# V in SBUF at 136 instead of 130 bf16 per key chunk, in an attention and MLP kernel on one core

## The chip, the cores and the metric

The kernel runs on one core of a Trainium2 chip. The metric is the time of one execution on the device, in microseconds (us); the median of three runs is given with its lowest and highest. A core has engines that run side by side: PE (matrix products; it loads one operand, the weights, into its array, which the profile lists as PEld, and streams the other one through), DVE (vector work), ACT (activation functions), POOL and SP (here mostly issuers of DMAs). Data lie in SBUF, which has 128 partitions, and PE writes its results to PSUM.

## What is computed

```python
# x (1, 2048, 576), k_cache and v_cache (1, 16, 2048, 128), all bf16
xn = layernorm(x)
# A: 32 query heads on 16 key heads, of the last W = 512 keys
q = (xn @ wq) as 32 heads of 128
scores = q @ k.T * 128 ** -0.5
p = softmax(scores)
o = p @ v
s = o as (2048, 4096) @ wo
# B: an MLP block with a token shift
h = gelu(layernorm(xn) @ w1); hs = shifted(h) @ w2; x1 = xn + hs
b = x1 + gelu(layernorm(x1) @ w3) @ w4
out = x + s * silu(b)
```

## The kernel before

The 2048 tokens are cut into 4 query blocks of 512 (QB, NB). A unit u is one query block and one of the 32 query heads, so there are 128 units; two query heads share a key head g = (u % 32) // 2. The 512 keys of a key head are 4 chunks kc of 128 (KCH).

Attention is a loop over the units. In it `stage_q` makes the queries of the next unit (line 439, with a remainder at 425 from the second block on), `stage_s` the scores of this unit, chunk by chunk (line 459), from which ACT makes the exponentials pT in bf16 (line 461; a pool of 10 tiles), and `stage_v` weighs V for the unit before (line 476). For every token tile of 128, `stage_v` adds four matmuls, kc 0 to 3, into one place of `po`: the weights are a 128x128 piece of pT, and the streamed operand is 129 columns of V, of which the last is ones, so that column 128 of the result is the sum of the exponentials. The first of the four overwrites, the others add. Two token tiles share one `po` tile (2 of them, PSUM), so a call is eight matmuls, and there are 2 calls a unit, 256 in all, 2048 matmuls. DVE then takes the reciprocal of the sums and multiplies (lines 480, 481), and a DMA transposes the outcome (line 489).

Between these, PE is given pieces of other work by unit: transposes of K (line 297), the output projection of the block before (line 500, into `pswo` 512 columns wide and `pswr` 64 wide), and the first half of the MLP (lines 552 and 603). After the loop come the output projection of the last block, and the second half of the MLP (lines 849, 886 and, at the end, 1049 and 1069). The order on PE, POOL and SP in the attention part is the order of the program; the order on ACT and DVE is made by the framework's planner, which is told of some priorities.

V is kept in `v_sb`, one tile for all 16 key heads (line 215): on each partition 16 x 4 chunks of VW values, VW = Dh + 2 = 130 (line 77). A chunk's first 128 values are filled by DMA, 256 bytes a row (`load_v`, line 287): the first two calls on SP's queue at the start, the other six on POOL's, each eight units ahead of its first use. The remaining VW - 128 values of every chunk are set to 1.0 once, on POOL, at the start (line 330). `stage_v` reads values 0 to 128 of a chunk (line 477). On POOL the fills of line 331 to 333 (w1r_sb, w1_sb and w2_sb) and the V loads stand behind line 330.

```python
v_sb = res.tile([P, Hkv, KCH, VW], BF16, name="v_sb")                       # 215
nc.gpsimd.memset(v_sb[:, :, :, Dh:VW], 1.0)                                  # 330
nc.tensor.matmul(po[:, j, :], lhsT=pTs[kc][:, tt * P:(tt + 1) * P],          # 476
                 rhs=v_sb[:, g, kc, 0:Dh + 1], start=(kc == 0), stop=(kc == KCH - 1))
```

Of the kernel before, what the change touches and what calls it, by code (L numbers as in the profile page):

```python
# [31 lines left out]
def kernel(  # L32
# [19 lines left out]
    _, Hkv, Sk, Dh = A_k_cache.shape  # L52
# [21 lines left out]
    rsz = c4 - P  # L74
    SHIFT = [1, -1, 2, -2]
    PAD = 2
    VW = Dh + 2
    HP = 1500

    x2 = A_x.rearrange("b s d -> (b s) d")  # L80
# [127 lines left out]
    with ExitStack() as actx:  # L208
# [5 lines left out]
        kT = res.tile([P, Hkv, W], BF16, name="kT")  # L214
        v_sb = res.tile([P, Hkv, KCH, VW], BF16, name="v_sb")
        NWQ = 2
# [60 lines left out]
        def load_k(i, eng=None, step=4):  # L277
            kst_t[i] = x1_pool.tile([P, TB, D], BF16, name="x1")
            dst = kst_t[i][:].rearrange("p a b -> p (a b)")[:, 0:4 * W].rearrange("p (g a) -> p g a", g=4)
            for g in range(0, 4, step):  # L280
                (eng or nc.gpsimd).dma_start(
                    out=dst[:, g:g + step, :],
                    in_=A_k_cache[0, 4 * i + g:4 * i + g + step, K0:, :].rearrange("g (p kc) d -> p g (kc d)", p=P))
# [39 lines left out]
        with tc.manual_schedule(engines={SP}):  # L323
# [5 lines left out]
            load_k(1, nc.sync)  # L329
        nc.gpsimd.memset(v_sb[:, :, :, Dh:VW], 1.0)  # L330
        nc.gpsimd.memset(w1r_sb[:], 0.0)
# [866 lines left out]
```

## Time and profile before

| | us |
|---|---|
| median of three runs (lowest, highest) | 837.76 (837.19, 838.02) |
| profiled execution, its time | 837.62 |
| its span, first to last instruction | 835.8 |
| attention loop, first to last V matmul start | 15.4 to 514.0 |
| second half of the MLP on PE, from | 545.8 |

The granted clock of PE was 0.998 over the span. The profile is of one execution. Its page gives busy time by engine, the span in 40 slices with busy tenths, the costliest groups (line, engine, operation, result<-operands, shape, count, then busy us and the mean ns of one, then the engine's idle time ahead of them and what ended most of it), and the DMA queues. The trace also answers with a list of waits (engine, line and the event waited for: us in total, times, longest), with a timeline, where neighbouring instructions of one line are put together (start us, length us, count), and with windows (for a stretch: busy us of each engine, PE's clock, DMA share, GB/s). A matmul's length there is its passage through the array's pipeline, in which the next one already runs; how fast matmuls follow each other is read from their starts. A few records of matmuls are missing, none of line 476's.

### The profile page before, as it was taken

How to read it: one execution, taken by the hardware profiler on the slowest of the kernel's cores; microseconds unless marked ns; L12 is line 12 of the kernel's file. 1: busy time of each engine (PE TensorE's matmuls, PEld its weight loads, DVE VectorE, ACT ScalarE, POOL GpSimd, SP SyncE). 2: the span in 40 equal slices, each digit the busy share in tenths (PEclk: the TensorE clock that was granted, in tenths of full speed). 3: DMA queues.
4: the chain of work that ended last, by engine and by line, in shares of the span. 5: the costliest groups of instructions: out<-in, count | busy, mean ns of one | idle time of the engine just before them, and what ended most of it. 6: DMA issues, size and time to landing. Idle time of an engine off the chain costs nothing.

```text
span 835.8 us, 19469 instructions
## 1 busy us (share of the span) xinstructions
PE 820.3 (98%) x7885; PEld 475.9 (57%) x7971; DVE 473.8 (57%) x1430; ACT 452.9 (54%) x806; POOL 91.8 (11%) x157
## 2 busy tenths in 40 slices
PE   8999999999999999999999999999999999999997
PEld 5666654665554466655465655455555555555555
DVE  5778655568794366965346774044245636645333
ACT  6777763488783368984357983033332433334610
POOL 3242323011110101110000100000000000000000
PEclk9999999999999999999999999999999999999999
DMA  7988992263473135762035464992001411230101
GB/s 186 198 160 196 189 181 74 62 116 92 90 150 62 42 88 125 132 130 60 13 80 120 103 107 73 305 346 53 2 3 43 81 52 44 47 87 16 44 15 46
DMA packets 140752, 83.95 MB, mean 100 GB/s; under 512 B 107328, under 2 KB 133632, under 8 KB 140656
## 3 DMA queue, kind: packets, MB, share of 16 engines
q1 hardware_dynamic: 130048, 53.01, 31.3%
q0 software_dynamic: 9216, 28.15, 12.7%
q8 instruction: 64, 1.05, 0.6%
q10 hardware_dynamic: 1392, 1.48, 0.5%
q14 instruction: 32, 0.26, 0.1%
HBM read 49.17 MB, written 9.44 MB: 70 GB/s over the span
## 4 chain that ended last, share of the span: by engine, by line


## 5 line engine op out<-in xcount | busy, mean ns | idle before, releaser
L461 ACT ACTIVATE pT<-sc 128x512 bf16<-128x512 f32 x512 | 288.9, 596 | 116.1 <-PE sc L459 105.5
L459 PE MATMUL sc<-qT,kT 128*128 128x512 bf16 x493 | 169.0, 378 | 0.9 <-DVE qT L449 0.6
L476 PEld LDWEIGHTS <-pT 128*128 128x128 bf16 x2048 | 137.7, 98 | 53.7 <-issue 7.6
L476 PE MATMUL po<-v_sb,pT 128*128 128x129 bf16 x2048 | 161.7, 220 | 1.3 <-ACT pT L461 0.3
L439 PE MATMUL psq<-xT_b,wq_b 128*128 128x512 bf16 x509 | 134.3, 379 | 2.1 <-DVE xT_b L405 0.3
L849 PE MATMUL ph<-xT_b,w_s 64*128 64x512 bf16 x976 | 127.1, 376 | 0.2 <-DVE hx L865 0.2
L886 PE MATMUL pm<-w_s,h 64*128 64x512 bf16 x864 | 122.3, 377 | 0.0
L500 PE MATMUL pswo<-wo_sb,oT 128*128 128x512 bf16 x500 | 115.4, 379 | 0.8
L481 DVE TENSOR_TENSOR o<-po,ri_b 128x256 bf16<-128x256 f32 x256 | 107.8, 421 | 6.1
L867 ACT ACTIVATE h<-ph 128x512 bf16<-128x512 f32 x67 | 39.4, 597 | 130.3 <-PE ph L849 130.3
L886 PEld LDWEIGHTS <-h 64*128 64x128 bf16 x1728 | 70.8, 94 | 55.6 <-issue 0.4
L500 PEld LDWEIGHTS <-oT 128*128 128x128 bf16 x1024 | 65.2, 98 | 57.1 <-DMA oT<-o 0.6
L886 PE MATMUL pr<-w_s,h 64*128 64x64 bf16 x864 | 90.2, 189 | 0.2 <-ACT h L867 0.2
L439 PEld LDWEIGHTS <-wq_b 128*128 128x128 bf16 x544 | 52.8, 97 | 62.9 <-issue 1.9
L849 PEld LDWEIGHTS <-w_s 64*128 64x128 bf16 x1152 | 57.2, 94 | 48.6 <-issue 0.5
L865 DVE COPY hx<-ph 128x512 f32<-128x512 f32 x55 | 38.0, 691 | 69.7 <-PE ph L849 69.7
L480 DVE RECIPROCAL ri_b<-po 128x2 f32<-128x2 f32 x256 | 42.4, 166 | 47.0 <-PE po L476 42.1
L449 DVE CAST qT<-psq 128x512 bf16<-128x512 f32 x56 | 38.6, 689 | 43.5 <-PE psq L425 23.8
L459 PEld LDWEIGHTS <-kT 128*128 128x128 bf16 x512 | 47.0, 97 | 24.5 <-DVE qT L449 0.6
L264 POOL DMA_DIRECT2D wq_b<-in_A_wq_dram x30 | 23.2, 774 | 298.3 <-PE sc L459 283.1
L447 DVE TENSOR_TENSOR qT<-psq,rq 128x512 bf16<-128x512 f32 x48 | 33.1, 690 | 18.9 <-ACT pT L461 10.4
L839 DVE TENSOR_SCALAR fence<-ph,ph 1x1 f32<-1x1 f32 x61 | 12.8, 209 | 50.6 <-PE ph L849 50.0
(146 smaller groups left out, 731.9 us busy)
## 6 DMA issues: line engine op xcount, KB each, us to landing
wq_b<-in_A_wq_dram POOLq DMA_DIRECT2D x30, 512.0 KB, 4.8
w_s<-in_B_w_dram SPq DMA_DIRECT2D x9, 576.0 KB, 7.1
wo_sb<-in_A_wo_dram POOLq DMA_DIRECT2D x8, 576.0 KB, 5.4
w_s<-in_B_w_dram SPq DMA_DIRECT2D x9, 512.0 KB, 7.9
x_dram<-x SPq DMA_DIRECT2D x4, 576.0 KB, 3.4
x<-x_dram SPq DMA_DIRECT2D x4, 576.0 KB, 4.3
s_b<-s_dram SPq DMA_DIRECT2D x4, 576.0 KB, 5.5
x_b<-in_A_x_dram SPq DMA_DIRECT2D x4, 576.0 KB, 6.3
```

The source lines that it names most:

```text
L439: nc.tensor.matmul(psq[:, :], lhsT=w[:, kc, hh * Dh:(hh + 1) * Dh], rhs=xT_b[qb % 2][:, kc, :], start=(kc == 0 and not (qb and hh == 1)), ...
L449: nc.vector.tensor_copy(out=qT[:, :], in_=psq[:, :])
L459: nc.tensor.matmul(sc[:, :], lhsT=kT[:, g, kc * P:(kc + 1) * P], rhs=qT_t[u][:, :], start=True, stop=True)
L461: nc.scalar.activation(out=pT[:, :], in_=sc[:, :], func=ACT.Exp, scale=SCALE)
L476: nc.tensor.matmul(po[:, j, :], lhsT=pTs[kc][:, tt * P:(tt + 1) * P], rhs=v_sb[:, g, kc, 0:Dh + 1], start=(kc == 0), stop=(kc == KCH - 1))
L480: nc.vector.reciprocal(out=ri, in_=po[:, :, Dh])
L481: nc.vector.tensor_tensor(out=o[:, t0:t0 + 2, :], in0=po[:, :, 0:Dh], in1=ri.unsqueeze(2).to_broadcast([P, 2, Dh]), op=ALU.mult)
L500: nc.tensor.matmul(ps, lhsT=oT_t[qb * Hq + h][:, tt, :], rhs=wo_sb[:, h, lo:hi], start=(h == 0), stop=(h == Hq - 1))
L849: nc.tensor.matmul(ps[i][:, :], lhsT=lhsT, rhs=xT[half, kc, :], start=first, stop=last, skip_group_check=True)
L865: nc.vector.tensor_copy(out=src[:, :], in_=ps[i][:, :])
L867: nc.scalar.activation(out=h3[:, :], in_=src[:, :], func=ACT.Gelu_apprx_tanh)
L886: nc.tensor.matmul(out, lhsT=h3_t[b, fc][half, tt * P:(tt + 1) * P], rhs=w4_s[fc // WS][half, fc % WS, lo:hi], start=key not in started, s ...
```

## The change

One constant: a key chunk of V takes Dh + 8 = 136 values (272 bytes) of a partition instead of Dh + 2 = 130 (260 bytes). The tile grows from 64 x 260 = 16,640 to 64 x 272 = 17,408 bytes a partition. The fill of line 330 writes 8 instead of 2 values of each chunk. The matmuls read the same 129 values of each chunk as before, and the DMAs write the same 128.

```diff
     SHIFT = [1, -1, 2, -2]
     PAD = 2
-    VW = Dh + 2
+    VW = Dh + 8
     HP = 1500
```

## The prediction

> **What bounds the kernel now.** I read the page first: the busy table, the busy tenths, and the two costliest groups of the attention part.
>
> ```profile
> span 835.8 us, 19469 instructions
> PE 820.3 (98%) x7885; PEld 475.9 (57%) x7971; DVE 473.8 (57%) x1430; ACT 452.9 (54%) x806; POOL 91.8 (11%) x157
> ...
> PE   8999999999999999999999999999999999999997
> ...
> ACT  6777763488783368984357983033332433334610
> ...
> L461 ACT ACTIVATE pT<-sc 128x512 bf16<-128x512 f32 x512 | 288.9, 596 | 116.1 <-PE sc L459 105.5
> ...
> L476 PE MATMUL po<-v_sb,pT 128*128 128x129 bf16 x2048 | 161.7, 220 | 1.3 <-ACT pT L461 0.3
> ```
>
> PE is at 9 in every slice but the first and the last, and ACT, the next engine in the attention part (15 to 514 us), idles 116 us ahead of its exponentials, 105.5 of it until PE has delivered scores. Second, the list of waits, PE's own rows; all of them together are under 5 us, and only the last two here belong to the attention loop, one at its start (13.3 us) and one at its end (512.8 us).
>
> ```profile
> PE warm L747 <- POOL ident masks.py:199: 1.6, 1, 1.6
> PE ps_k L297 <- DMA x<-in_A_k_cache_dram: 1.1, 1, 1.1
> ...
> PE sc L459 <- ACT pT L461: 0.3, 1, 0.3
> PE po L476 <- ACT pT L461: 0.3, 1, 0.3
> ```
>
> So from 15 us on the end is set by how fast PE streams its matmuls, one after the other. The 2048 matmuls that read V (line 476) are part of that stream, and a nanosecond on each is 2 us at the end.
>
> Third, what one of them costs. The 220 ns of the group is the time through the pipeline; the price is the distance from one start to the next. The timeline of PE, in three short stretches (start, length, line, form, count):
>
> ```profile
> 303.73 0.63 PE L476 MATMUL po<-v_sb,pT 128*128 128x129 bf16 x8
> 304.20 0.38 PE L459 MATMUL sc<-qT,kT 128*128 128x512 bf16 x1
> ...
> 541.95 3.90 PE L500 MATMUL pswr<-wo_sb,oT 128*128 128x64 bf16 x128
> ...
> 824.91 3.13 PE L1049 MATMUL pm<-w_s,h 128*128 128x192 bf16 x36
> 827.88 0.21 PE L1069 MATMUL pm<-x,ident 128*128 128x96 bf16 x1
> ```
>
> Eight V matmuls take 304.20 - 303.73 = 0.47 us, 58.7 ns each. For comparison: 36 of 192 columns take 827.88 - 824.91 = 2.97 us, 82.5 ns each; 128 of 64 columns take (3.90 - 0.19)/127 = 29.2 ns each, with 0.19 us for the last one's own passage. The line through both is 0.416 ns a column and 2.6 ns fixed, so 129 columns should take 56.3 ns. The V matmuls are 2.4 ns above that, on average.
>
> Fourth, where the 2.4 ns sit. All 2048 records are there, in program order: each eight is two token tiles times key chunks kc 0, 1, 2, 3. I took from the trace, to the nanosecond, the distance from each start to the next matmul's, left out distances over 66 ns (a wait, or an unrecorded matmul between), and averaged by chunk: kc 0 56.05 ns, kc 1 60.14, kc 2 59.25, kc 3 59.31 (482 to 512 values each). A chunk is now 260 bytes and a head 1040 = 65 x 16, so against a multiple of 16 kc 0 lies at 0, and kc 1, 2, 3 at 4, 8, 12 bytes, in every head, counted from the first byte of the tile. The chunk that lies at a multiple of 16 is the one that runs at the 56.3 of the line; the three others pay 3 to 4 ns more.
>
> **The change part by part.** *Matmuls.* Their count and shape stay: they read columns 0 to 128 of a chunk as before. With 272 = 17 x 16 bytes a chunk, kc 1, 2, 3 come into the class of kc 0, wherever the tile begins. Against 64 bytes the new chunks lie at 0, 16, 32, 48; kc 0 of the heads has all four of these today (1040 g leaves 16 g), and its mean is 56.0 to 56.1 in each. The price of the other three becomes 56.05: the gain is 512 x (4.09 + 3.20 + 3.26) = 512 x 10.55 ns = 5.40 us. Bounds: nothing (they stay as they are), and 512 x 11.2 ns = 5.8 us if they go to the 55.8 ns that kc 0 of the second token tile shows, which has no wait ahead of it.
>
> The Trainium skill (page "SBUF — State Buffer", Specifications, cachelines) speaks against this: memory lines have 16 bytes, and each crossing to a new line costs. A row of 258 bytes touches 17 such lines from offset 0, and also from 4, 8 and 12, so by counting lines alone the four chunks would cost the same and the change would bring nothing; the trace's 56.05 against 59.2 to 60.1 doesn't agree with counting alone.
>
> *Does it reach the end?* PE waits for nothing in the loop today, so what is late next is ACT. Windows of four heads in its densest part and over the loop (PE, PEld, DVE, ACT, POOL busy):
>
> ```profile
> 341.00:352.30 11.30, 11.19 (x99) 6.89 (x100) 10.24 (x38) 10.26 (x20) 3.15 (x5) 1.00 0.92 160
> ...
> 15.40:514.50 499.10, 494.41 (x4189) 293.51 (x4266) 329.25 (x1034) 340.30 (x614) 84.38 (x139) 1.00 0.54 109
> ```
>
> Four heads have 64 V matmuls, 48 of them dearer: 4 x 4 x 10.55 = 169 ns saved, 11.30 becomes 11.13 us, with ACT at 10.26. It fits, with 0.87 us to spare, DVE (10.24) likewise. ACT is as dense as this in about 167 to 250, 317 to 386 and 449 to 507 us, some 210 of the loop's 499; if it could not follow in any of them, 5.40 x 210/499 = 2.3 us would be lost. I take no loss. After the loop come the last output projection, weight loads issued after the last transpose, and the MLP, none of which reads V; they begin earlier by what the loop saves.
>
> *The ones column's fill* (line 330, POOL) writes 64 x 8 instead of 64 x 2 values:
>
> ```profile
> 2.87 0.22 POOL L330 MEMSET v_sb<- 128x128 bf16 x1
> 3.02 0.64 POOL L331 MEMSET w1r_sb<- 128x640 bf16 x1
> ```
>
> By the neighbouring rows (128x256 0.30 to 0.32, 64x512 0.52, 128x640 0.64) it becomes some 0.5 us, +0.3; bounds 0 and +0.42. Behind it on POOL stand three more fills (w1 and w2, loaded from head 26 on) and, at 4.87 us, the issue of V loads for heads that start after 25 us; these land in 8.6 us at most. Nothing reads the ones before the first V matmul at 15.4. So nothing on the path; uncovered it would cost 0.3 us once.
>
> *V loads* (16 issues of 128 KB, POOL and SP): as many rows of 256 bytes, to other places. No row shows the new price; their landings of 4.1 to 8.6 us bound what could be won, and a doubling, to 17 us, would still lie inside the eight heads (over 20 us) between issue and use; the first, issued at 3.8 us for use at 15.4, would stand at 12 us even with its 8.6. Nothing either way. *Space*: 64 x 12 = 768 bytes more a partition; tiles laid behind it move by three times 256 bytes and keep their place against 256.
>
> Sum: -5.40 us. The profiled execution has 837.62 us (span 835.8 and 1.8 around it), 0.14 under the median 837.76 of three runs that lie 0.8 apart; on that median 837.76 - 5.40 gives 832.3 (-0.65%).
>
> **The rivals.** *B, no change, 837.6.* The extra goes with something else that parts kc 0 from the rest: kc 0 is also the one that overwrites po, and kc 1 to 3 add to it. In these 2048 the two can't be told apart. Against it: the chains above of 64 and 192 columns add into the same place matmul after matmul and lie, with the 512-column ones (215 to 216 ns, the line gives 215.6), on one line without extra. A cost by the number of 16-byte pieces would end here too: 17 in each chunk before and after, so 2048 matmuls at today's prices, 0.00 us saved. (This is the Trainium skill's line rule, page "SBUF — State Buffer", Specifications.) Chance 0.08, of which 0.02 for counting.
>
> *C, slower, 839.7.* The extra comes from the V read meeting the read of the next weights (pT), by their places against each other, and kc 0 escapes by its place among four different ones. With all four chunks alike, kc 0 pays the 60.1 of kc 1 too: 512 x 4.09 = +2.1 us; it is slower by over 0.2% from 1.7 us / 4.09 ns = 415 such matmuls on. For it: it too makes a difference by kc. Against: pT turns through 10 buffers with four tiles a head, so that a chunk doesn't keep its partner, while its price holds to 0.5 ns over all 16 heads; and the 64-column chains load new weights every 29 ns without extra. Chance 0.05.
>
> *D, the gain given back in part, 834.6.* ACT's exponentials bound the dense stretches: -5.40 + 2.3 = -3.1. For it 91% busy there; against, that PE's waits for it are 0.6 us in all, and that ACT idles until scores come in each unit of work. Chance 0.07.
>
> **How the numbers follow.** Forecast 0.80, B 0.08, C 0.05, D 0.07. About 0.2% (1.7 us) is what a measurement of this kernel can tell from no change. Forecast and D are faster by more: 0.87; B is the same: 0.08; C slower: 0.05. The predicted time is the forecast's, 832.3. The range runs from 831.2 (all 5.8 us, and 0.7 for the spread of the runs) up to 834.9, which takes in D; B and C and the tails, under 2 in 10, are left out.
>
> **What would show it.** In the changed kernel's trace the starts of V matmuls should be 56 ns apart for every chunk, eight of them in 0.45 instead of 0.47 us, and the loop's end (the last V matmul, at 514.0 us) should come at about 508.6. Equal prices at 56 with an unchanged end would mean a new wait on ACT (D); kc 1 to 3 still at 59 to 60 mean B; kc 0 at 60, C. The fill of the ones should be near 0.5 us and followed by no PE wait. The forecast is wrong if the distance by chunk doesn't follow the byte offset, or if ACT's and DVE's own order changes so that PE gets waits that the list above doesn't have.

## The result, and the profile after

| us | before | after |
|---|---|---|
| median, all runs (lowest, highest) | 837.76 (837.19, 838.45), 19 runs | 834.44 (833.97, 838.0), 19 runs |
| profiled execution, its span | 837.62, 835.8 | 834.87, 833.1 |
| first V matmul to last V matmul, starts | 15.41 to 513.97: 498.56 | 15.34 to 510.76: 495.42 |
| last V matmul to last matmul of the kernel | 315.44 | 315.60 |

The kernel became faster by 0.36%: ratio 0.9964, 95% interval 0.9957 to 0.9971. The medians lie 3.3 us apart where 5.4 had been forecast. The span of the profiled execution fell by 2.7 us. The attention loop alone became 3.1 us shorter; what lies ahead of it and behind it became longer by some 0.5 us together.

The page of the changed kernel, the same rows as before:

```profile
span 833.1 us, 19467 instructions
PE 817.5 (98%) x7885; PEld 472.8 (57%) x7971; DVE 473.4 (57%) x1430; ACT 452.2 (54%) x806; POOL 92.3 (11%) x157
...
L461 ACT ACTIVATE pT<-sc 128x512 bf16<-128x512 f32 x512 | 288.5, 598 | 113.5 <-PE sc L459 104.4
...
L476 PE MATMUL po<-v_sb,pT 128*128 128x129 bf16 x2048 | 158.2, 220 | 1.3 <-ACT pT L461 0.3
```

PE is as busy as it was, and the V matmuls' own busy time fell from 161.7 to 158.2 us. (Busy time counts overlapping passages once, so it follows the distances, while the 220 ns of one passage stay.) PE's waits in the changed kernel:

```profile
PE ps_k L297 <- DMA x<-in_A_k_cache_dram: 0.6, 1, 0.6
...
PE pswo L500 <- DMA oT<-o: 0.3, 1, 0.3
PE po L476 <- ACT pT L461: 0.3, 1, 0.3
PE sc L459 <- ACT pT L461: 0.3, 1, 0.3
```

One is new, 0.3 us in the last output projection (line 500), which needs the last transposes; in the runs below that keep the order 0, 1, 2, 3 it is between nothing and 0.6 us, so it isn't tied to this change. The first, before the loop, was 1.1. And the timeline of PE, with the eight V matmuls of one call:

```profile
301.93 0.62 PE L476 MATMUL po<-v_sb,pT 128*128 128x129 bf16 x8
302.38 0.59 PE L459 MATMUL sc<-qT,kT 128*128 128x512 bf16 x2
```

Eight take 302.38 - 301.93 = 0.45 us instead of 0.47. To the nanosecond, averaged over the trace as in the prediction, the distances from kc 0, 1, 2, 3 to the next start are now 56.68, 56.66, 56.66 and 56.68 ns (before: 56.05, 60.14, 59.25, 59.31). So the four chunks became alike, as forecast, but at 56.67 and not at the 56.05 that kc 0 had; kc 0 itself became dearer. Four cost 226.7 ns instead of 234.7.

### The profile page after: what moved, and what is told of

It is laid out like the page before. It is cut to its first block, busy times and chain, and to the rows that moved or that the text cites. A ratio compares the mean times of both kernels' runs of the same rounds, so it can differ in the third digit from the quotient of the medians.

```text
span 833.1 us, 19467 instructions
## 1 busy us (share of the span) xinstructions
PE 817.5 (98%) x7885; PEld 472.8 (57%) x7971; DVE 473.4 (57%) x1430; ACT 452.2 (54%) x806; POOL 92.3 (11%) x157
## 4 chain that ended last, share of the span: by engine, by line
## 5 line engine op out<-in xcount | busy, mean ns | idle before, releaser
L476 PEld LDWEIGHTS <-pT 128*128 128x128 bf16 x2048 | 135.0, 98 | 53.6 <-issue 7.6
L476 PE MATMUL po<-v_sb,pT 128*128 128x129 bf16 x2048 | 158.2, 220 | 1.3 <-ACT pT L461 0.3
```

## The experiments

Three theories of the extra are told apart. A, the prediction's: a V matmul is dear when its read begins off a multiple of 16 bytes. E: it is dear when its read begins at another place against 16 than the read before it. F came up after the first four runs: it is dear when its read begins in the same 16 bytes (counted from a multiple of 16) in which the V matmul just before it ended its read. At pitch 260, kc 0 reads bytes 0 to 257 and kc 1 begins at 260: both touch 256 to 271, and kc 2 and 3 follow kc 1 and 2 in the same way.

**All four chunks at 4, at 8, at 16 bytes past a multiple of 16.** One edit, with N = 2, 4, 8 values:

```diff
-        v_sb = res.tile([P, Hkv, KCH, VW], BF16, name="v_sb")
+        v_sb = res.tile([P, Hkv * KCH * VW + 16], BF16, name="v_sb")[:, N:N + Hkv * KCH * VW].rearrange("p (g k w) -> p g k w", g=Hkv, k=KCH)
```

> The changed kernel's pitch of 272 bytes, with the whole of V begun 4 bytes (2 values) later, so that all four chunks lie 4 bytes past a multiple of 16. Theory A (the extra goes with the place of the streamed read against 16 bytes): every chunk dear, at the 59.3 ns that a chunk behind another dear one had before; four cost 237 ns against 226.7 in the changed kernel, 512 x 10.4 = +5.3 us, some 0.3 given back by the aligned matmul that follows, so 839.5 us (about 1.002 of the kernel before). Theory E (the extra comes from the change of place between neighbours, 0 to 4 to 8 to 12): no change of place, 56.7 ns each and 834.4 us. Theory B (the extra goes with adding instead of overwriting) is already against the changed kernel's trace; it would give 834.4.

> As the run before it, with V begun 8 bytes later: all four chunks 8 past a multiple of 16. Theory A with 16 bytes as the unit: 839.5 us, every V matmul at about 59.3 ns. Theory A with 8 bytes as the unit, or Theory E: 834.4 us and 56.7 ns.

> As the two before it, with V begun 16 bytes later: tile size and neighbours are theirs, the chunks lie at multiples of 16 again. Every theory here: 834.4 us as the changed kernel, 56.7 ns a V matmul. A time like that of the 4-byte run would mean that it is the larger tile or its start, not the place against 16, that costs.

Measured, with the ratio to the kernel before and its interval: 834.67 (0.9951, 0.9929 to 0.9973), 835.1 (0.9945, 0.9924 to 0.9965) and 834.7 us (0.9946, 0.9924 to 0.9969); loops (first to last V matmul) of 495.40, 495.40 and 495.45 us; every chunk's mean between 56.6 and 56.7 ns. The page's rows of the V matmuls are, for the 4-byte run,

```profile
L476 PE MATMUL po<-v_sb,pT 128*128 128x129 bf16 x2048 | 158.2, 220 | 1.3 <-ACT pT L461 0.3
```

and the same 158.2 in the other two. Theory A falls: reads that begin 4 or 8 bytes off a multiple of 16 cost nothing when all do. What the change put right was not that.

**A pitch of 264 bytes.** `VW = Dh + 4`.

> A pitch of 132 values, 264 bytes: kc 0 and 2 at a multiple of 16, kc 1 and 3 at 8 past it. Theory A, 16 bytes: dear behind cheap costs 60.1 ns, cheap behind dear 56.05, so four cost 232.4 against 234.75 before: 512 x 2.4 = 1.2 us less than before, 836.5 us. With 8 bytes as the unit: 834.4. Theory E: each neighbour changes its place, so as before or worse, 837.8 or more.

Measured: 838.44 us, ratio 0.9992 (0.9965 to 1.0019), with runs from 835.81 to 844.31: the time decides nothing. The trace does: the distances are 56.1, 60.2, 55.8, 59.3 ns, kc 1 and 3 dear as A had it, and the loop 497.46 us, 1.10 under the kernel before. E, by which each chunk should have been dear, falls with this one and with the first two (a score matmul, whose streamed tile is taken to begin at a multiple of 16, is followed by a V read at 4 or 8 there); the run at 276 bytes below speaks against it too. What fits this and the first three is F: at 264, kc 1 begins at 264 where kc 0 ended at 257 (both in 256 to 271); kc 2 begins at 528 where kc 1 ended at 521 (not in one 16); kc 3 shares again.

**F tried at the old pitch, by order alone.** The kernel before, with `for i, kc in enumerate((0, 2, 1, 3))` and then `(3, 2, 1, 0)` in `stage_v`, start and stop set by i. No read begins in the 16 bytes in which the last one ended. The other way round some do share: in 3, 2, 1, 0 every read behind kc 3 ends in the 16 bytes in which the one before it began, and in 0, 2, 1, 3 kc 1 does so behind kc 2, which the expectation overlooks.

> The kernel before, pitch 260, with the four chunks taken in the order 0, 2, 1, 3 (the sum over keys in another order). Theory F (a V matmul is dear when its read begins in the same 16 bytes in which the matmul just before it ended its read: at pitch 260 kc 1, 2, 3 after kc 0, 1, 2): no successive reads share 16 bytes, so all four at 56.7 ns and 834.4 us, the changed kernel's time with none of its layout. Theory A (the place of the read against a multiple of 16): as before, kc 1 to 3 at 59 to 60 ns and 837.8 us. Theory E (change of place between neighbours): 0, 8, 4, 12 change at each step, 837.8 us.

> The kernel before, pitch 260, chunks in the order 3, 2, 1, 0. Here a read ends in the 16 bytes in which the one before it began. Theory F, only the step from an end to a start counts: 56.7 ns each and 834.4 us. If sharing 16 bytes with the read before counts in any way: dear as before, 837.8 us. Theories A and E: 837.8 us.

Order 0, 2, 1, 3: 834.99 us (six runs), ratio 0.9965 (0.9952 to 0.9978), loop 495.50 us: the gain of the change, to within 0.1 us of the loop, without a byte of the new layout. The page's row of the V matmuls in this kernel:

```profile
L476 PE MATMUL po<-v_sb,pT 128*128 128x129 bf16 x2048 | 158.2, 219 | 1.3 <-ACT pT L461 0.3
```

The expected 56.7 ns for each was a miss: in the order of execution the distances are 56.2, 58.9, 55.8, 56.4. One distance is longer and others are shorter; the sum is 227.3, against 226.7 in the changed kernel. Order 3, 2, 1, 0: the sum is 227.2, but the time 837.59 us (835.81 to 856.05), ratio 0.9998 (0.9985 to 1.0012), so by time nothing was gained. The list of PE's waits in that kernel shows a part of the loss:

```profile
PE pswo L500 <- DMA oT<-o: 0.8, 1, 0.8
...
PE po L476 <- ACT pT L461: 0.4, 1, 0.4
```

The last unit's first V matmul now needs the exponentials that come last. The loop has 495.95 us and the stretch from the last V matmul to the last matmul 316.43, together 1.4 us more than in the changed kernel. That fits the execution that was traced, 835.98 us; what lifts the median to 837.59 the trace doesn't show. To see whether the order itself did this, it was run with the new pitch too, where no reads share 16 bytes either way round:

> The changed kernel (pitch 272 bytes) with the chunks in the order 3, 2, 1, 0. No two successive reads of V share 16 bytes in any way. In the run of this order at pitch 260 the time didn't fall as its V matmuls did. If that lay in the order itself (the last unit's first matmul now needs the exponentials that come last, and the output projection behind it waits for the last transpose): V matmuls at 56.67 ns throughout, but the same waits of 0.4 us at line 476 and some 0.8 us at line 500, a loop of 495.7 us and a lowest time near 835.8. If it lay in reads that share 16 bytes the other way round: 495.4 us, waits of 0.3 us, and 834.4 us as the changed kernel.

Measured: 836.43 us, ratio 0.9987 (0.9978 to 0.9996), lowest 835.58; 56.65 to 56.67 ns for each chunk, loop 495.74 us, waits of 0.4 us at line 476 and 1.1 at line 500, loop and the stretch behind it again 1.4 us above the changed kernel's. So these 1.4 us come with the order, at the end of the loop and behind it, not with the reads. Why the medians lie 1.8 us (pitch 260) and 0.9 us (pitch 272) above the lowest times stays open.

**F tried with old places, and with one shared step only.** `VW = Dh + 10` (276 bytes: places 0, 4, 8, 12 as in the kernel before, no shared 16) and `VW = Dh + 6` (268 bytes: only kc 0 to kc 1 share).

> The changed kernel with a pitch of 138 values, 276 bytes: the chunks lie at 0, 4, 8, 12 past a multiple of 16, as in the kernel before, but 18 bytes lie between one chunk's read and the next, so that none shares 16 bytes with its neighbour. Theory F: 56.7 ns each, 834.4 us. Theories A and E: 59 to 60 ns for kc 1 to 3, 837.8 us.

> The changed kernel with a pitch of 134 values, 268 bytes: chunks at 0, 12, 8, 4 past a multiple of 16; kc 0 ends at byte 258 and kc 1 starts at 268 (both in 256 to 271), kc 1 ends at 526 and kc 2 starts at 536 (512 to 527, 528 to 543), kc 2 ends at 794 and kc 3 starts at 804 (784 to 799, 800 to 815). Theory F: kc 1 alone is dear, 60.1 ns, kc 2 56.05, kc 3 and 0 56.7: four cost 229.5 against 226.7, +1.5 us on the changed kernel, 835.9 us. Theories A and E: kc 1 to 3 dear, 837.8 us.

Pitch 276: 834.47 us, ratio 0.9967 (0.9949 to 0.9984), loop 495.42 us; distances 56.7, 58.3, 55.8, 55.9, so not 56.7 for each as expected, but their sum is 226.7. Pitch 268: 836.55 us, ratio 0.9994 (0.9972 to 1.0016), so by time undecided between F and A; loop 496.28 us; distances 56.4, 60.9, 55.8, 55.9, kc 1 alone dear, as F has it, sum 229.0. The row of the V matmuls on the pages of the three pitches, a line each. First the kernel at 264 bytes, with two shared steps (busy us, then the mean passage):

```profile
L476 PE MATMUL po<-v_sb,pT 128*128 128x129 bf16 x2048 | 160.0, 220 | 1.3 <-ACT pT L461 0.3
```

The same row of the kernel at 268 bytes, with one:

```profile
L476 PE MATMUL po<-v_sb,pT 128*128 128x129 bf16 x2048 | 159.1, 220 | 1.3 <-ACT pT L461 0.3
```

And of the kernel at 276 bytes, with none; busy time falls by about one us a step from 161.7 with three:

```profile
L476 PE MATMUL po<-v_sb,pT 128*128 128x129 bf16 x2048 | 158.1, 219 | 1.3 <-ACT pT L461 0.3
```

The kernels by the number of steps, of the three between four chunks, in which a read begins in the 16 bytes in which the last one ended:

| shared steps | kernel | distances in order of execution, ns | sum | busy, us | loop, us |
|---|---|---|---|---|---|
| 3 | before, 260 | 56.0 60.1 59.2 59.3 | 234.7 | 161.7 | 498.56 |
| 2 | 264 | 56.1 60.2 55.8 59.3 | 231.4 | 160.0 | 497.46 |
| 1 | 268 | 56.4 60.9 55.8 55.9 | 229.0 | 159.1 | 496.28 |
| 0 | after, 272 | 56.7 56.7 56.7 56.7 | 226.7 | 158.2 | 495.42 |
| 0 | 272, begun 4 bytes later | 56.7 56.6 56.7 56.7 | 226.7 | 158.2 | 495.40 |
| 0 | 276 | 56.7 58.3 55.8 55.9 | 226.7 | 158.1 | 495.42 |
| 0 | 260, order 0 2 1 3 | 56.2 58.9 55.8 56.4 | 227.3 | 158.2 | 495.50 |
| 0 | 260, order 3 2 1 0 | 58.4 56.2 56.2 56.3 | 227.2 | 158.2 | 495.95 |
| 0 | 272, order 3 2 1 0 | 56.7 56.7 56.7 56.7 | 226.6 | 158.0 | 495.74 |

Sum, busy time and loop fall with the count, whatever the places are (in the two kernels with the order 3, 2, 1, 0 the loop has the wait at its end besides). The 16 comes out of these runs too: with 8 bytes as the unit, kc 2 at pitch 260 would not share with kc 1 (byte 517, then 520), yet it is dear; with 32, kc 2 at pitch 264 would (521, then 528), yet it is cheap. Three steps fewer take 234.7 - 226.7 = 8.0 ns from the sum, 2.7 a step, and 3.14 us from the loop, 2.0 ns for each of 1536 steps.

**One column more, and a smaller fill.** Two terms of the changed kernel: 56.67 ns are 0.42 above the 56.25 of a straight line through the other widths, one column's worth; and the fill of line 330 writes seven values nobody reads.

```diff
-            po = ps_po.tile([P, 2, Dh + 1], FP32, name="po", tag="po")
+            po = ps_po.tile([P, 2, Dh + 2], FP32, name="po", tag="po")
...
-                                     rhs=v_sb[:, g, kc, 0:Dh + 1], start=(kc == 0), stop=(kc == KCH - 1))
+                                     rhs=v_sb[:, g, kc, 0:Dh + 2], start=(kc == 0), stop=(kc == KCH - 1))
```

```diff
-        nc.gpsimd.memset(v_sb[:, :, :, Dh:VW], 1.0)
+        nc.gpsimd.memset(v_sb[:, :, :, Dh:Dh + 1], 1.0)
```

> The changed kernel with 130 instead of 129 columns of V streamed by each of the 2048 matmuls (one more column of ones, which nothing reads). In the changed kernel each takes 56.67 ns, where the line through the widths 64, 192 and 512 gives 56.25 for 129 and 56.67 for 130 columns. If an odd width is paid as the next even one: 56.67 ns, the loop's 495.4 us from first to last V matmul and 834.4 us. If 0.42 ns of the 56.67 are left from the reads of V and a column costs 0.417: 57.1 ns, +0.85 us in the loop.

> The changed kernel with the fill of line 330 cut to the one value of each chunk that is read (the seven others stay unset and unread). The fill took 0.22 us before and 0.53 after. If it costs nothing at the end, as the prediction has it: the loop's 495.4 us and 834.4 us, with line 330 at some 0.2 us. If the 0.3 us reach the end: 834.1.

130 columns: 834.89 us, ratio 0.9959 (0.9939 to 0.998), loop 495.46 us, 56.7 ns each. The page's row:

```profile
L476 PE MATMUL po<-v_sb,pT 128*128 128x130 bf16 x2048 | 158.2, 220 | 0.3 <-ACT pT L461 0.3
```

The same 158.2 as with 129: 129 columns are paid as 130, and 56.67 is what the line gives for 130, so nothing is left of the reads' extra in the changed kernel. The small fill: 834.86 us, ratio 0.9959 (0.994 to 0.9978), loop 495.41 us. The fill took 0.39 us there, a miss against the 0.2 expected, and 0.53 in the changed kernel. POOL's timeline with the small fill:

```profile
2.88 0.39 POOL L330 MEMSET v_sb<- 128x64 bf16 x1
```

No difference at the end shows.

## Why the prediction was right, and where it was not

*The bound.* Right: the loop follows PE's stream, matmul by matmul. The fill (0.5 us forecast, 0.53 measured), the V loads and the space cost nothing that a run showed.

*The class of the price.* Right that kc 1 to 3 were dear and would become cheap; wrong in the reason. "Against a multiple of 16" and "the three come into the class of kc 0" described a coincidence: at pitch 260 the chunks off a multiple of 16 are also those that begin in the 16 bytes in which the last read ended. The runs at 4 and 8 bytes, and at 276, have the first without the second, and pay nothing; with the order 0, 2, 1, 3 at pitch 260 all but 0.6 of the 8.0 ns are gone. Rivals B and C fell with the changed kernel's trace: adding matmuls run at 56.67 there, and with all four chunks alike none is at 60. The part of B that counts 16-byte pieces fell with the time: the reads touch as many pieces as before, and the kernel became faster.

*The size.* This is the step that failed: "The price of the other three becomes 56.05: the gain is 512 x 10.55 ns = 5.40 us". The loop gained 3.14. Three parts of the gap can be read from the starts of the matmuls in the two traces (the same few records are missing in both).

- The price of kc 0 in the kernel before was not the price of a cheap matmul among cheap ones. A distance runs from start to start, and behind a dear matmul a cheap one comes out short: 55.8 to 56.1 ns in the rows before, 264 and 268 of the table above. The steady price is 56.67, which is that of 130 columns. With it, three chunks gain 3.47, 2.58 and 2.64 ns and kc 0 loses 0.62: 8.07 ns x 512 = 4.1 us.
- The 512-wide matmuls had come out short in the same way: a score matmul behind V matmuls took 215.0 ns before and takes 215.9 after. Over the loop's 512-wide ones that is 0.35 us.
- ACT is met, as rival D had it, but in a few places, and DVE is met too. Where three score matmuls stand together, the third waits for ACT: in 16 of these places it starts 50 to 52 ns after the end of an exponential (line 461), before and after. The distance ahead of it was 7 to 10 ns over 215.8 and is now 23 to 24, together 0.24 us. One such three before (start, length of all three, count):

```profile
300.88 0.81 PE L459 MATMUL sc<-qT,kT 128*128 128x512 bf16 x3
```

and the same three after:

```profile
299.09 0.83 PE L459 MATMUL sc<-qT,kT 128*128 128x512 bf16 x3
```

In two other places the first score matmul of a head waits for its queries, which DVE writes (line 447): it starts 57 to 60 ns after that instruction's end. One distance went from 79 to 174 ns over 215.8, and one of 86 over is new, together 0.18 us. The one of 79 in the timeline of the kernel before; the last line is the load of the waiting matmul's weights:

```profile
359.17 0.68 DVE L447 TENSOR_TENSOR qT<-psq,rq 128x512 bf16<-128x512 f32 x1
...
359.62 0.69 PE L459 MATMUL sc<-qT,kT 128*128 128x512 bf16 x2
...
359.91 0.10 PEld L459 LDWEIGHTS <-kT 128*128 128x128 bf16 x1 [0.25 <-DVE qT L447]
```

and the same place in the timeline of the changed kernel:

```profile
356.97 0.68 DVE L447 TENSOR_TENSOR qT<-psq,rq 128x512 bf16<-128x512 f32 x1
...
357.32 0.78 PE L459 MATMUL sc<-qT,kT 128*128 128x512 bf16 x2
...
357.71 0.10 PEld L459 LDWEIGHTS <-kT 128*128 128x128 bf16 x1 [0.34 <-DVE qT L447]
```

Two score matmuls in a row take 0.59 us where nothing is waited for; here 0.69, and 0.78 in the changed kernel. The starts in the loop add up: line 476 gives 4.06 us, the other 512-wide matmuls take back 0.35, the waits 0.42, and the half-height matmuls of line 425, the transposes of K and the 64-wide ones 0.15, which leaves 3.14.

So "PE waits for nothing in the loop today" was not quite so: short waits for ACT and DVE were there before. They are not in the list of PE's waits, since the passage of the matmul ahead, some 380 ns, still counts as busy while the next one is late. D's bound of 2.3 us took every dense stretch as lost; the 0.87 us that four heads have to spare on average was in fact there, except at these places, and rival D named ACT alone.

*The Trainium skill's line rule* (page "SBUF — State Buffer", Specifications) gives lines of 16 bytes. The unit agrees with the runs: at 268 bytes the same ten bytes part kc 0's last byte from kc 1's first and kc 1's last from kc 2's first, and only the step inside one 16 is dear. The count of lines per read, which would have left the time as it was, is not what sets the price here.

What stays open is what the array or the memory does in such a step; the runs show when it costs, and how much. Open too are the 0.5 and 0.6 ns by which the orders 3, 2, 1, 0 and 0, 2, 1, 3 at the old pitch stay above the changed kernel in the sum of four, and why single distances at 276 bytes differ while their sum is the changed kernel's. No version tried beats the changed kernel; the one with the old pitch and the order 0, 2, 1, 3 reaches its time within the intervals and saves 768 bytes a partition.

## What to carry to other kernels

Where narrow matmuls (129 bf16 columns here; no other width was tried) follow each other and stream neighbouring pieces of one tile, let the next read not begin in the 16 bytes in which the last one ended: pad the pitch, or take the pieces in another order. The price here was 2.3 to 3.3 ns of some 57 for each such step. When a price is taken from one member of a repeating group, take it from the sum over the group: the distance of a single matmul holds part of its neighbour's cost. And look for short waits in the starts: a matmul can be late while its engine still counts as busy.

## What the runs showed of the hardware that was not expected

- A matmul of 129 streamed columns costs as much as one of 130: 56.67 ns from start to start for both, and the same 158.2 us of busy time for 2048.
- Streamed bf16 reads that begin 4 or 8 bytes off a multiple of 16 cost nothing when no two share 16 bytes: loops of 495.40 us against 495.42.
- A streamed read that begins in the 16 bytes in which the one before ended costs 2.7 ns more over the four matmuls, per step (8.0 for three); ten bytes apart across a multiple of 16 costs nothing (268 bytes, kc 1 to kc 2).
- A POOL fill of one bf16 value in every 272 bytes took 0.39 us for 64 values, and of eight of them 0.53 for 512.
